# Two heads' key-value products in alternation on 64-column halves, with one shared 128-row tile for their last tokens

## The chip, the cores and the metric

The kernel runs on one core of a Trainium2 chip. The metric is device time in microseconds; the kernel before takes 1699.87 us, the median of three runs (1699.16 to 1702.06). Float32 throughout. TensorE (PE) multiplies and writes to PSUM, VectorE (DVE), ScalarE (ACT) and GpSimd (POOL) do the rest, and SyncE (SP) issues the transfers.

## The reference

Eight batches of eight heads with 576 tokens of 64 features go through a softmax attention without a score matrix, and its output through two layers:

```
q_s = exp(q - max(q over features));  q_s = q_s / (sum over features + 1e-9)
k_s = exp(k - max(k over tokens));    k_s = k_s / (sum over tokens + 1e-9)
kv  = k_s^T v            (64 x 64 for each batch and head, summed over 576 tokens)
x   = q_s kv             -> (4608 tokens, 512)
x   = relu(x w_in)^2 w_out      (512 -> 2048 -> 512)
out = silu(x w_in2) w_out2      (512 -> 2048 -> 512)
```

The change concerns `kv` alone: the product of the exponentials of k with v, and how the last 64 of the 576 tokens are laid out for it.

## The kernel before

Tokens go in nine blocks of 512, through the first layer block by block (phase 0) and then through the second (phase 1). In either phase a block has 16 slots, one for each chunk of 128 hidden features. `layer_in` (lines 397 to 404) makes the 12 products of a chunk of the first matrix, and `layer_out` (lines 448 to 470) those of the second, two chunks behind. All of these are float32r products of 128 rows, 128 columns and 512 moving columns.

The attention of batch and block b + 1 runs beside block b of phase 0, head pair by head pair. Pair 0 to 3 starts at slot 0, 4, 8 and 11: its k, q and v are loaded one slot earlier, the maximum over tokens and the exponential follow in slots 0 and 1 of its own, and `kv_mm` (lines 210 to 218) two slots behind the start. Batch 0 has all this ahead of the layers, in an order written out by hand (`first_loads`, `first_steps`), with its tiles in room that later weights take (`spare`). A scheduler then orders each engine's instructions, so neighbours in the code need not be neighbours on the engine.

`kv_load` (lines 148 to 175) lays the first 512 tokens of two heads on 128 partitions, 4 tokens each (`kk`), and the last 64 on 64 partitions, the two heads side by side (`krr`, 64 x 128). v has the same layout, with a column of ones behind each head's 64 features (`vv`, `vrr`), so that the product gives the sum of the exponentials too. `kv_max` takes the maximum over a partition's tokens, then over partitions on GpSimd (line 196); `kv_exp` subtracts it and takes exp (lines 201 to 206).

`kv_mm` sums a head's five products in one PSUM tile: four over 128 rows (line 216) and one over the 64 rows of the last tokens (line 217). Head 0 has PSUM partitions 0 to 63, which are TensorE's columns 0 to 63, head 1 the other half. Head 0's five go first, then head 1's. `kv_norm` follows on VectorE and ScalarE.

What sets the order around it: SyncE's queue runs in order, and from the ninth transfer on each waits for one issued eight earlier. GpSimd's queue runs in order as well. The k, v and last-token tiles of later batches have one buffer each, so loads and memsets of a pair wait for the products of the pair before. PSUM tiles of the attention share two buffers.

Of the kernel before, what the change touches and what calls it, by code (L numbers as in the profile page):

```python
# [19 lines left out]
def f32(ap):  # L20
    """A float32r tile's values, read as the float32 numbers that they are."""
    return ap.bitcast(F32)
# [3 lines left out]
def kernel(  # L26
# [10 lines left out]
):  # L37
    """softmax attention -> relu^2 layer -> silu layer, in float32.

    The weights come as the words of float64 numbers (zero, or of a size within float32's normal  # L40
    range) and are rounded to the nearest float32 here.

    A float32 x is the exact sum of two float32r numbers, hi = round(x) to 12 significant bits and
    lo = x - hi. The big products are hi*hi + hi*lo + lo*hi, each an exact one-pass product that
    PSUM sums in float32; lo*lo lies below float32's rounding.

    Tokens go in blocks of 512, as columns: column 128 * a + 32 * r + j of a block is its token
    128 * a + 4 * j + r, which softmax has on partition 32 * a + j.
    Activations stay transposed (features on partitions) until the last product.
    """  # L50
    nc = tc.nc
    P = 128
# [9 lines left out]
    SR = S - SM  # L62
    # (block, pair) whose q softmax leans on ScalarE, while the weights keep VectorE busy.
    ON_ACT = ((0, 0), (0, 1), (0, 2), (1, 0), (1, 1), (1, 2), (1, 3))
    EPS = 1e-9
    Q = 32
    # Blocks whose q goes through TensorE to be transposed.
    PE_TR = (0, 1)
# [22 lines left out]

# [1 line left out]
    w_in = (w_in1, w_in2)  # L93
# [20 lines left out]
    def round_w(ph, f, which):  # L114
        """float64 words -> the nearest float32's bits."""
        t = raw.pop((ph, f, which))
        lw, hw = t[:, :, 0], t[:, :, 1]
        u = tpool.tile([P, DM], I32, tag="wu", name="wu")
        nc.scalar.activation(lw, lw.bitcast(U32), AF.Copy, scale=2.0 ** -29)  # L119
        nc.vector.tensor_scalar(  # L120
            u, hw, 0x07FFFFFF, 3, op0=ALU.bitwise_and, op1=ALU.logical_shift_left
        )
        nc.vector.scalar_tensor_tensor(  # L123
            u, hw, -0x40000000, u, op0=ALU.bitwise_and, op1=ALU.bitwise_or
        )
        nc.vector.tensor_tensor(u, u, lw, op=ALU.add)  # L126
        raw[ph, f, which] = u
# [10 lines left out]

# [1 line left out]
    kt, krt, vt, vrt, mt, mbt = {}, {}, {}, {}, {}, {}  # L140

    def spare(pr, j):
        """Room of the last weights, which block 0's attention can have."""
        n = 6 * pr + j
        tag = f"wo{'hl'[n % 2]}{NF - 1 - n // 2}"
        return wpool.tile([P, TB], F32, tag=tag, name=f"spare{n}")

    def kv_load(b, pr):
        hs = slice(2 * pr, 2 * pr + 2)
        if b == 0:  # L150
            t = [spare(pr, j) for j in range(4)]
            kk, krr = t[0], t[3][0:SR, 0:2 * D]
            w = R * (D + 1)
            vv = [t[1][:, 0:w], t[2][:, 0:w]]
            vrr = t[1][0:SR, w:w + 2 * (D + 1)]
            m, mb = t[3][:, 2 * D:4 * D], t[3][:, 4 * D:6 * D]
        else:
            kk = apool.tile([P, TB], F32, tag="k", name="k")
            krr = apool.tile([SR, 2 * D], F32, tag="kr", name="kr")
            t = apool.tile([P, 2, R * (D + 1)], F32, tag="v", name="v")  # L160
            vv = [t[:, 0, :], t[:, 1, :]]
            vrr = apool.tile([SR, 2 * (D + 1)], F32, tag="vr", name="vr")
            m = apool.tile([P, 2 * D], F32, tag="m2", name="m2")
            mb = apool.tile([P, 2 * D], F32, tag="mb", name="mb")
        kk = kk.rearrange("p (h r d) -> p h r d", h=2, r=R)
        krr = krr.rearrange("p (h d) -> p h d", h=2)
        vv = [x.rearrange("p (r d) -> p r d", r=R) for x in vv]
        vrr = vrr.rearrange("p (h d) -> p h d", h=2)
        nc.sync.dma_start(out=kk, in_=k[b, hs, 0:SM, :].rearrange("h (p r) d -> p h r d", r=R))
        nc.sync.dma_start(out=krr, in_=k[b, hs, SM:S, :].rearrange("h p d -> p h d"))  # L170
        for j in range(2):
            nc.gpsimd.memset(vv[j][:, :, D:D + 1], 1.0)
        nc.gpsimd.memset(vrr[:, :, D:D + 1], 1.0)
        kt[b, pr], krt[b, pr], vt[b, pr], vrt[b, pr] = kk, krr, vv, vrr
        mt[b, pr], mbt[b, pr] = m, mb

    def v_load(b, pr):
        hs = slice(2 * pr, 2 * pr + 2)
        for j in range(2):
            nc.sync.dma_start(  # L180
                out=vt[b, pr][j][:, :, 0:D],
                in_=v[b, 2 * pr + j, 0:SM, :].rearrange("(p r) d -> p r d", r=R),
            )
        nc.sync.dma_start(
            out=vrt[b, pr][:, :, 0:D], in_=v[b, hs, SM:S, :].rearrange("h p d -> p h d")
        )

    def kv_max(b, pr):
# [5 lines left out]
        nc.vector.tensor_tensor(m2, m1[:, :, 0, :], m1[:, :, 1, :], op=ALU.max)  # L194
        nc.vector.tensor_tensor(m2[0:SR], m2[0:SR], tr, op=ALU.max)
        nc.gpsimd.partition_all_reduce(mb, m, P, bass_isa.ReduceOp.max)

    def kv_exp(b, pr):
# [4 lines left out]
        )  # L203
        nc.vector.tensor_tensor(tr, tr, mb[0:SR], op=ALU.subtract)
        nc.scalar.activation(t, t, AF.Exp)
# [4 lines left out]
    def kv_mm(b, pr):  # L210
        ps = ps_a.tile([P, D + 1], F32, tag="a", name="kvps")
        ek, ekr, va, vr = kt.pop((b, pr)), krt.pop((b, pr)), vt.pop((b, pr)), vrt.pop((b, pr))
        for j in range(2):
            o = ps[D * j:D * j + D]
            for r in range(R):
                nc.tensor.matmul(o, ek[:, j, r, :], va[j][:, r, :], start=(r == 0), stop=False)  # L216
            nc.tensor.matmul(o, ekr[:, j, :], vr[:, j, :], start=False, stop=True)  # L217
        kvps[b, pr] = ps
# [17 lines left out]
    def pieces(i):  # L236
        """(batch, first and last partition) of block i's tokens."""
        got, p = [], 0
# [62 lines left out]
    def q_tr(i, pr):  # L301
        t = qt.pop((i, pr))
        if i in PE_TR:
# [5 lines left out]
            return  # L309
        # VectorE transposes blocks of 32 x 32 in their place; a trip through DRAM orders them.  # L310
        u = t.rearrange("p h r d -> p (h r d)")
# [9 lines left out]
    def parts(t, p0, p1):  # L321
        """The columns of a block's tokens on partitions p0 to p1."""
        got = []
# [26 lines left out]
    def x_mm(i, pr):  # L350
        hi, lo = qht.pop((i, pr), None), qlt.pop((i, pr), None)
        got = []
        for b, s, p0, p1 in pieces(i):
# [4 lines left out]
            else:  # L358
                # A float32r product runs at full rate from 256 columns on.
                c0, c1 = p0 // Q * P, -(-p1 // Q) * P  # L360
# [9 lines left out]

# [1 line left out]
    xh = [xpool.tile([P, TB], F32R, name=f"xh{c}") for c in range(KC)]  # L372
# [20 lines left out]

# [1 line left out]
    gh, gl, gf, acc = {}, {}, {}, {}  # L395
# [29 lines left out]
    def evict(ph, i, e, last):  # L425
        """A finished accumulator to DRAM; the kernel's last ones in two halves side by side."""
        w = TB // 2 if last else TB
        for n in range(TB // w):
# [3 lines left out]
            if ph == 0:  # L432
                # Phase 1's columns: r * 128 + p for token 4 * p + r.
                to = t.rearrange("p (r a j) -> p a r j", r=R, j=Q)
                have = have.rearrange("p (a r j) -> p a r j", r=R, j=Q)
# [12 lines left out]
    def layer_out(ph, i, fn):  # L448
        """Adds the products of some chunks, (f, n) each, to block i's four accumulators."""
        ended = fn[-1][0] == NF - 1  # L450
# [20 lines left out]

# [1 line left out]
    side = {}  # L473
# [42 lines left out]
    items = [(ph, i, f) for ph in range(2) for i in range(NB) for f in range(NF)]  # L516
    # Each chunk's second product runs two chunks behind its first.
    order = []
# [14 lines left out]

    # Weights, (phase, chunk, in or out), in the order in which they are needed.
    wlist = [(0, 0, 0), (0, 1, 0)]
# [3 lines left out]

    # Block 0's attention and the first weights: a letter code and a pair (or a weight) each, loads  # L540
    # first, then the steps by their priority.
    code = dict(
# [39 lines left out]
    for what, n in order:  # L582
        ph, i, f = items[n]
        if what == "in":
# [14 lines left out]
            hidden_lo(n)  # L599
            # Phase 1's weights take the places of phase 0's as its last block lets them go.  # L600
            slot = n - (NB - 1) * NF
# [42 lines left out]
```

## Time and profile before

| what | value |
|---|---|
| median of three runs | 1699.87 us |
| span of the profiled execution | 1697.9 us |
| median less that span | 2.0 us |
| PE busy | 1671.6 us, 98% |
| DVE, ACT, POOL busy | 712.6, 606.0, 42.2 us |
| line 216, with the batches' own tiles | 448 records, 38.0 us |
| line 217, the same | 112 records, 18.2 us |
| first product on PE | 19.95 us |
| last product of line 217 | 710.4 us |

Busy times of PE overlap: a record covers the way of a product through the array, so the distance from one start to the next is what a product costs in a row, not its duration. A float32 product shows as two records of MATMUL and two of LDWEIGHTS (PEld, the load of the stationary operand). Shapes are rows times columns of the array used: 128*64 is 128 rows and half of the columns.

### The profile page before, as it was taken

To read this page: it belongs to the slowest core of one execution; us is meant where nothing else is said; L and a number is where in the kernel's file an instruction comes from. 1 tells how busy PE (TensorE), PEld (TensorE's weight loads), DVE (VectorE), ACT (ScalarE), POOL (GpSimd) and SP (SyncE) were. 2 spreads that over 40 slices of the span, in tenths; PEclk is the share of its full clock that TensorE was granted. 3 is DMA by queue.
4 is the path that set the end of the run, shared out by engine and by line. 5 is a ranking of instruction groups with operands and counts; after the bars stand their busy time and mean duration, and the time that the engine had idled before them with its cause. 6 is when DMAs were issued, how large, how long until landed. Compare 5 with 4: busy or idle time off the path is not lost.

```text
span 1697.9 us, 20340 instructions
## 1 busy us (share of the span) xinstructions
PE 1671.6 (98%) x7768; PEld 1373.7 (81%) x7768; DVE 712.6 (42%) x1393; ACT 606.0 (36%) x1186; POOL 42.2 (2%) x148
## 2 busy tenths in 40 slices
PE   5999999999999999999999999999999999999999
PEld 3878888888888888888887888888888888888887
DVE  6997565555656555553686121212121212121211
ACT  6785333332333233332565232223232323222222
POOL 1010000000000000000000000000000000000000
PEclk9999999999999999999999999999999999999999
DMA  6664221231222122120454010101010101010000
GB/s 178 199 202 131 73 72 52 57 93 54 77 66 73 57 70 77 37 81 13 126 170 138 0 50 0 50 1 50 0 50 0 50 1 50 1 50 1 15 11 25
DMA packets 119842, 106.19 MB, mean 63 GB/s; under 512 B 49600, under 2 KB 98752, under 8 KB 119744
## 3 DMA queue, kind: packets, MB, share of 16 engines
q1 hardware_dynamic: 119744, 104.89, 20.1%
q8 instruction: 61, 1.00, 0.2%
q14 instruction: 37, 0.30, 0.1%
HBM read 78.64 MB, written 26.21 MB: 62 GB/s over the span
## 4 chain that ended last, share of the span: by engine, by line
PE 94%; DVE 2%; DMA 2%; ACT 1%; issue 0%; SPq 0%; POOL 0%; DVEq 0%; ACTq 0%
PE acc L463 44%; PE h L401 15%; PE h L402 15%; PE h L403 15%; PE kvps L216 2%; DMA wraw<-in_moe_w_out_dram 1%; PE kvps L217 1%; PE xps L367 1%; PE xps L366 1%; PE xps L365 1%; DMA wraw<-in_moe_w_in_dram 0%; DVE wu L126 0%; DVE wu L123 0%; ACT wraw L119 0%; PE qps L307 0%
## 5 line engine op out<-in xcount | busy, mean ns | idle before, releaser
L422 DVE TENSOR_TENSOR gl<-g,gh 128x512 fp32r<-128x512 f32 x288 | 198.9, 691 | 637.8 <-ACT gh L417 635.3
L401 PE MATMUL h<-xh,wih 128*128 128x512 f32 x1152 | 448.5, 390 | 0.6 <-ACT g L416 0.6
L402 PE MATMUL h<-xl,wih 128*128 128x512 f32 x1152 | 449.0, 390 | 0.0
L403 PE MATMUL h<-xh,wil 128*128 128x512 f32 x1152 | 448.8, 390 | 0.0
L416 ACT ACTIVATE g<-h 128x512 f32<-128x512 f32 x144 | 86.1, 598 | 521.5 <-PE h L403 521.5
L401 PEld LDWEIGHTS h<-xh,wih 128*128 128x128 f32 x1152 | 216.0, 188 | 46.9 <-ACT g L416 1.0
L402 PEld LDWEIGHTS h<-xl,wih 128*128 128x128 f32 x1152 | 216.3, 188 | 45.6 <-DVE xl L378 0.4
L403 PEld LDWEIGHTS h<-xh,wil 128*128 128x128 f32 x1152 | 216.2, 188 | 45.6 <-DVE wil L135 0.4
L463 PE MATMUL acc<-gh,woh 128*128 128x512 f32 x576 | 228.0, 396 | 0.0
L463 PE MATMUL acc<-gl,woh 128*128 128x512 f32 x576 | 224.8, 390 | 1.0 <-DVE gl L422 0.9
L463 PE MATMUL acc<-gh,wol 128*128 128x512 f32 x576 | 224.7, 390 | 0.0
L463 PE MATMUL acc<-woh,gh 128*128 128x512 f32 x576 | 224.1, 389 | 0.0
L463 PE MATMUL acc<-wol,gh 128*128 128x512 f32 x576 | 224.1, 389 | 0.0
L463 PE MATMUL acc<-woh,gl 128*128 128x512 f32 x576 | 224.1, 389 | 0.0
L417 ACT CAST gh<-g 128x512 fp32r<-128x512 f32 x288 | 178.8, 621 | 60.1 <-DVE g L414 53.7
L410 ACT ACTIVATE g<-h 128x512 f32<-128x512 f32 x144 | 85.6, 594 | 260.4 <-PE h L403 259.9
L414 DVE TENSOR_TENSOR g<-g 128x512 f32<-128x512 f32 x112 | 77.3, 690 | 201.8 <-ACT g L410 201.1
L463 PEld LDWEIGHTS acc<-gh,woh 128*128 128x128 f32 x576 | 108.1, 188 | 23.0 <-ACT gh L417 0.3
L463 PEld LDWEIGHTS acc<-gh,wol 128*128 128x128 f32 x576 | 108.1, 188 | 22.8
L463 PEld LDWEIGHTS acc<-woh,gl 128*128 128x128 f32 x576 | 108.1, 188 | 22.6
L463 PEld LDWEIGHTS acc<-woh,gh 128*128 128x128 f32 x576 | 108.2, 188 | 22.4
L463 PEld LDWEIGHTS acc<-gl,woh 128*128 128x128 f32 x576 | 108.2, 188 | 22.4 <-DVE gl L422 1.8
(100 smaller groups left out, 1150.9 us busy)
## 6 DMA issues: line engine op xcount, KB each, us to landing
wraw<-in_moe_w_in_dram SPq DMA_DIRECT2D x32, 512.0 KB, 3.8
wraw<-in_moe_w_out_dram SPq DMA_DIRECT2D x32, 512.0 KB, 4.4
x2d<-ev SPq DMA_DIRECT2D x36, 256.0 KB, 2.1
xr<-x2d SPq DMA_DIRECT2D x36, 256.0 KB, 3.0
out_dram<-ev SPq DMA_DIRECT2D x32, 256.0 KB, 2.5
k<-in_k_dram SPq DMA_DIRECT2D x28, 256.0 KB, 2.8
v<-in_v_dram SPq DMA_DIRECT2D x56, 128.0 KB, 2.9
qd<-q SPq DMA_DIRECT2D x28, 256.0 KB, 2.0
```

The costliest lines, as they stand in the source:

```text
L216: nc.tensor.matmul(o, ek[:, j, r, :], va[j][:, r, :], start=(r == 0), stop=False)
L217: nc.tensor.matmul(o, ekr[:, j, :], vr[:, j, :], start=False, stop=True)
L365: nc.tensor.matmul(ps[:, o], wh, hi[:, o], start=True, stop=False)
L401: nc.tensor.matmul(h, wih[ph, f][o], xh[c], start=(c == 0), stop=False)
L402: nc.tensor.matmul(h, wih[ph, f][o], xl[c], start=False, stop=False)
L403: nc.tensor.matmul(h, wil[ph, f][o], xh[c], start=False, stop=(c == KC - 1))
L410: nc.scalar.activation(g, h, AF.Relu)
L414: nc.vector.tensor_tensor(g, g, g, op=ALU.mult)
L416: nc.scalar.activation(g, h, AF.Silu)
L417: nc.scalar.copy(hi, g)
L422: nc.vector.tensor_tensor(lo, gf.pop(n), f32(gh[n]), op=ALU.subtract)
L463: nc.tensor.matmul(acc[e], a, b, start=(f == 0 and j == 0), stop=(f == NF - 1 and j == 2))
```

## The change

The last 64 tokens of the two heads now share one tile of 128 partitions. v's has head 0 on partitions 0 to 63 and head 1 on 64 to 127, with one column of ones. k's has a block of 64 columns per head, and the other head's partitions in that block are filled with -3e38, which exp makes 0. So a head's product over all 128 rows adds nothing of the other head. Maxima, subtraction and exp run over all 128 partitions. Each of the two tiles is loaded by two transfers instead of one, and GpSimd fills the two padded quarters. In `kv_mm` the loop over the five products is the outer one now and that over heads the inner one. The rest of the textual difference is removed comments.

```diff
+    LOW = -3e38
...
         if b == 0:
-            kk, krr = t[0], t[3][0:SR, 0:2 * D]
+            kk, krr = t[0], t[3][:, 0:2 * D]
-            vrr = t[1][0:SR, w:w + 2 * (D + 1)]
+            vrr = t[1][:, w:w + D + 1]
...
-            krr = apool.tile([SR, 2 * D], F32, tag="kr", name="kr")
+            krr = apool.tile([P, 2 * D], F32, tag="kr", name="kr")
-            vrr = apool.tile([SR, 2 * (D + 1)], F32, tag="vr", name="vr")
+            vrr = apool.tile([P, D + 1], F32, tag="vr", name="vr")
...
+        for j in range(2):
+            nc.gpsimd.memset(krr[SR * j:SR * (j + 1), 1 - j, :], LOW)
         nc.sync.dma_start(out=kk, in_=k[b, hs, 0:SM, :].rearrange("h (p r) d -> p h r d", r=R))
-        nc.sync.dma_start(out=krr, in_=k[b, hs, SM:S, :].rearrange("h p d -> p h d"))
+        for j in range(2):
+            nc.sync.dma_start(out=krr[SR * j:SR * (j + 1), j, :], in_=k[b, 2 * pr + j, SM:S, :])
...
-        nc.gpsimd.memset(vrr[:, :, D:D + 1], 1.0)
+        nc.gpsimd.memset(vrr[:, D:D + 1], 1.0)
...
-        nc.sync.dma_start(
-            out=vrt[b, pr][:, :, 0:D], in_=v[b, hs, SM:S, :].rearrange("h p d -> p h d")
-        )
+        for j in range(2):
+            nc.sync.dma_start(
+                out=vrt[b, pr][SR * j:SR * (j + 1), 0:D], in_=v[b, 2 * pr + j, SM:S, :]
+            )
...
-        nc.vector.tensor_tensor(m2[0:SR], m2[0:SR], tr, op=ALU.max)
+        nc.vector.tensor_tensor(m2, m2, tr, op=ALU.max)
...
-        nc.vector.tensor_tensor(tr, tr, mb[0:SR], op=ALU.subtract)
+        nc.vector.tensor_tensor(tr, tr, mb, op=ALU.subtract)
...
-        for j in range(2):
-            o = ps[D * j:D * j + D]
-            for r in range(R):
-                nc.tensor.matmul(o, ek[:, j, r, :], va[j][:, r, :], start=(r == 0), stop=False)
-            nc.tensor.matmul(o, ekr[:, j, :], vr[:, j, :], start=False, stop=True)
+        for r in range(R + 1):
+            for j in range(2):
+                a, x = (ek[:, j, r, :], va[j][:, r, :]) if r < R else (ekr[:, j, :], vr)
+                nc.tensor.matmul(ps[D * j:D * j + D], a, x, start=(r == 0), stop=(r == R))
```

On PE, in block 1, the products of batch 2's first pair stand between `layer_in` (wih, wil) and `layer_out` (woh, wol) of a chunk. Before:

```order
L402 MATMUL h<-xl_129,wih_475 128x512
L403 MATMUL h<-xh_125,wil_476 128x512
L216 MATMUL kvps<-v,k 64x65 x4
L217 MATMUL kvps<-vr,kr 64x65
L216 MATMUL kvps<-v,k 64x65 x4
L217 MATMUL kvps<-vr,kr 64x65
L463 MATMUL acc_1713<-gh,woh_464 128x512
L463 MATMUL acc_1713<-gl,woh_464 128x512
```

The same place in the changed kernel, where the eight products over the first 512 tokens take the two heads in turn:

```order
L408 MATMUL h<-xl_129,wih_495 128x512
L409 MATMUL h<-xh_125,wil_496 128x512
L223 MATMUL kvps<-v,k 64x65 x8
L223 MATMUL kvps<-vr,kr 64x65 x2
L469 MATMUL acc_1749<-gh,woh_484 128x512
L469 MATMUL acc_1749<-gl,woh_484 128x512
```

The products of the last tokens stand together at the end now, and the whole keeps its place among the layers' products; so do all 24 pairs of batches 2 to 7.

On PE, in block 0, the last pair of batch 1, before:

```order
L463 MATMUL acc_617<-gl,woh_1257 128x512
L216 MATMUL kvps<-v,k 64x65 x4
L463 MATMUL acc_617<-gh,wol_1258 128x512
L217 MATMUL kvps<-vr,kr 64x65
L216 MATMUL kvps<-v,k 64x65 x4
L217 MATMUL kvps<-vr,kr 64x65
L463 MATMUL acc_618<-gh,woh_1257 128x512
```

And in the changed kernel:

```order
L469 MATMUL acc_636<-gh,woh_1367 128x512
L223 MATMUL kvps<-v,k 64x65 x8
L407 MATMUL h<-xh_122,wih_1378 128x512
L408 MATMUL h<-xl_126,wih_1378 128x512
L223 MATMUL kvps<-vr,kr 64x65 x2
L409 MATMUL h<-xh_122,wil_1379 128x512
```

Full-size products stand between the two parts of this pair in either kernel. Over batch 1's four pairs there are 6 such visits before (2, 1, 1 and 2) and 9 now (3, 2, 2 and 2).

## Rows read from the trace of the kernel before

**Rows 1.** The page's first part: busy time, share of the span, instructions.

```profile
PE 1671.6 (98%) x7768; PEld 1373.7 (81%) x7768; DVE 712.6 (42%) x1393; ACT 606.0 (36%) x1186; POOL 42.2 (2%) x148
```

**Rows 2.** The page's chain of work that ended last, by engine.

```profile
PE 94%; DVE 2%; DMA 2%; ACT 1%; issue 0%; SPq 0%; POOL 0%; DVEq 0%; ACTq 0%
```

**Rows 3.** Busy time by stretch: PE, PEld, DVE, ACT, POOL; clock, DMA share, GB/s.

```profile
120.00:230.00 110.00, 110.00 (x546) 90.11 (x545) 73.12 (x158) 46.84 (x89) 4.45 (x19) 1.00 0.35 101
...
670.00:780.00 110.00, 110.00 (x512) 90.59 (x512) 57.26 (x110) 36.22 (x68) 1.70 (x5) 1.00 0.18 57
```

**Rows 4.** The same view, a stretch of the first block.

```profile
60.00:80.00 20.00, 20.00 (x104) 16.35 (x103) 18.46 (x39) 16.49 (x43) 1.37 (x4) 1.00 0.59 191
```

**Rows 5.** PE's groups by form: count, busy us, mean ns, idle before.

```profile
L216 PE MATMUL kvps<-v,k 128*64 128x65 f32 x448 | 38.0, 227 | 0.2 <-issue 0.2
L217 PE MATMUL kvps<-vr,kr 64*64 64x65 f32 x112 | 18.2, 243 | 0.0
```

**Rows 6.** Timeline, one pair of batch 2: start us, us, engine, line, operation.

```profile
245.85 0.39 PE L402 MATMUL h<-xl,wih 128*128 128x512 f32 x1
...
246.07 0.39 PE L403 MATMUL h<-xh,wil 128*128 128x512 f32 x1
246.39 0.54 PEld L216 LDWEIGHTS kvps<-v,k 128*64 128x64 f32 x8 [0.35 <-issue]
246.39 0.68 PE L216 MATMUL kvps<-v,k 128*64 128x65 f32 x8
...
247.00 0.33 PE L217 MATMUL kvps<-vr,kr 64*64 64x65 f32 x2
...
247.26 0.68 PE L216 MATMUL kvps<-v,k 128*64 128x65 f32 x8
...
247.87 0.33 PE L217 MATMUL kvps<-vr,kr 64*64 64x65 f32 x2
...
248.12 0.50 PE L463 MATMUL acc<-gh,woh 128*128 128x512 f32 x1
...
248.69 0.39 PE L463 MATMUL acc<-gh,wol 128*128 128x512 f32 x1
```

**Rows 7.** The chain in order of time, a split pair of batch 1.

```profile
118.46 0.65 PE kvps L216 x8
119.11 0.43 PE acc L463
119.54 0.26 PE kvps L217 x2
```

**Rows 8.** PE's timeline, its first work (batch 0, first pair).

```profile
19.95 1.10 PE L216 MATMUL kvps<-spare,spare 128*64 128x65 f32 x8 [19.95 <-ACT spare L205]
20.97 0.47 PE L217 MATMUL kvps<-spare,spare 64*64 64x65 f32 x2
21.38 1.13 PE L216 MATMUL kvps<-spare,spare 128*64 128x65 f32 x8
```

**Rows 9.** POOL's timeline at the start.

```profile
0.73 0.14 POOL L172 MEMSET spare<- 128x4 f32 x2 [0.29 <-POOLq L627]
0.80 0.09 POOL L173 MEMSET spare<- 64x2 f32 x1
...
1.28 0.21 POOL L571 MEMSET kvf<- 128x128 f32 x1
...
17.52 2.23 POOL L196 PARTITION_ALL_REDUCE spare<-spare  x3 [6.46 <-issue]
```

**Rows 10.** SyncE's timeline at the start (SPq: an issue).

```profile
10.56 0.63 SPq L184 DMA_DIRECT2D spare<-in_v_dram  x1
...
15.05 0.59 SPq L101 DMA_DIRECT2D wraw<-in_moe_w_in_dram  x1
```

**Rows 11.** DVE's timeline: the second weight is taken up.

```profile
24.98 0.41 DVE L120 TENSOR_SCALAR wu<-wraw 128x512 int32<-128x512 int32 x1
```

**Rows 12.** Transfers of the first 40 us: count, size, median us to landing.

```profile
wraw<-in_moe_w_in_dram SPq DMA_DIRECT2D x4, 512.0 KB, 4.3
...
spare<-in_v_dram SPq DMA_DIRECT2D x4, 32.0 KB, 3.6
```

More of the change, by code (lines that the diff above doesn't have):

```diff
@@ L65 @@
     EPS = 1e-9
+    LOW = -3e38
+    assert 2 * SR == P
     Q = 32
@@ L167, in kv_load @@
         vv = [x.rearrange("p (r d) -> p r d", r=R) for x in vv]
-        vrr = vrr.rearrange("p (h d) -> p h d", h=2)
+        for j in range(2):
+            nc.gpsimd.memset(krr[SR * j:SR * (j + 1), 1 - j, :], LOW)
         nc.sync.dma_start(out=kk, in_=k[b, hs, 0:SM, :].rearrange("h (p r) d -> p h r d", r=R))
-        nc.sync.dma_start(out=krr, in_=k[b, hs, SM:S, :].rearrange("h p d -> p h d"))
+        for j in range(2):
+            nc.sync.dma_start(out=krr[SR * j:SR * (j + 1), j, :], in_=k[b, 2 * pr + j, SM:S, :])
         for j in range(2):
             nc.gpsimd.memset(vv[j][:, :, D:D + 1], 1.0)
-        nc.gpsimd.memset(vrr[:, :, D:D + 1], 1.0)
+        nc.gpsimd.memset(vrr[:, D:D + 1], 1.0)
         kt[b, pr], krt[b, pr], vt[b, pr], vrt[b, pr] = kk, krr, vv, vrr
@@ L177, in v_load @@
     def v_load(b, pr):
-        hs = slice(2 * pr, 2 * pr + 2)
         for j in range(2):
```

## The prediction

> **What bounds the kernel now.** I read the page first, by engine: TensorE (PE) is busy 98% of the span, VectorE 42%, ScalarE 36%, GpSimd 2% [rows 1]. The chain of work that ended last says the same, 94% of it on PE [rows 2]. Both are averages, so the table by stretches comes next: from 120 to 780 us, where the attention of the next batch runs beside the first layer, PE is busy 110.00 of every 110 us and VectorE 57 to 73 [rows 3]. Even in the first block, where the weights are rounded too, PE is full and VectorE stands at 18.46 of 20 us [rows 4]. So PE time removed between about 42 and 780 us is span removed, nearly one for one, and no other engine has to get faster for it.
>
> Then the rows of the touched lines. Line 216 has 512 MATMUL records (448 with the batches' own tiles, shown) and line 217 has 128 (112 shown) [rows 5]: 32 pairs of heads, 10 float32 products each, two passes to a product, 20 passes to a pair. The mean duration there (227, 243 ns) is useless as a price, since pipelined records overlap; starts are what counts. One undisturbed pair [rows 6]: the last full-size product starts at 246.07, then four runs start at 246.39, 247.00, 247.26 and 247.87, and the next full-size product at 248.12. Two runs of 8 passes take 0.61 each, two of 2 passes 0.255 on the mean. A straight line through these gives **p = 0.059 us per pass** ((0.61 - 0.255) / 6) and **s = 0.137 us per run** (0.255 - 2p). Four runs: 4 x 0.137 + 20 x 0.059 = 1.73, which is 248.12 - 246.39. So a run costs more than two passes before it does anything, and what starts a new run is the shape in the rows: 128*64 to 64*64 and back.
>
> A visit to this work costs something besides. From 246.07 to the third full-size start behind it, 248.69, is 2.62; three full-size steps (246.07 less the start before it, 245.85, hence 0.227) take 0.68 and the runs 1.73, which leaves **v = 0.21 us per visit** for leaving the full-size shape and coming back.
>
> **The change part by part.** *The runs.* All 20 passes of a pair now have 128 rows and 64 columns, so the shape changes only on entry and on exit: one run instead of four. The padded last tile costs no more passes (two per head, as before), and its 128 rows instead of 64 cost nothing in time per column: p fits both shapes above. What is new is that the output half changes after every product, 9 times a pair. No row shows a change of half without a change of shape. The nearest is from 247.00/247.26 [rows 6]: 217 of head 0 to 216 of head 1 changes both and takes as long (0.26) as 216 to 217, where the half stays. The half therefore added nothing that can be seen there. I take p for such a step; the bounds are half of p (both halves work at once) and p + s (it stalls like a change of shape). The saving is 3 x 0.137 = 0.41 us per pair. For batches 2 to 7, 24 pairs that stand in one piece before and after: **-9.8 us**.
>
> The Trainium skill, "TensorEngine Tiling (Array Packing)", Key Properties, says that a change of tiling mode, not merely of tile, drains TensorE. By that rule the three inner runs go and the nine half changes are free, which is the sum above; the s of the rows agrees with its first half, and no run here shows the second.
>
> *Batch 1* (its four pairs run in block 0). Here the order of the changed kernel is worse: the four pairs come in 9 visits instead of 6, since the late second transfer of the last k tokens makes the scheduler slip full-size products in between. Before: 16 runs, 6 visits, 80 passes: 16 x 0.137 + 6 x 0.21 + 80 x 0.059 = 8.17. Now: 9 runs, 9 visits: 9 x 0.137 + 9 x 0.21 + 4.72 = 7.84. **-0.3 us**. The trace has such a split at 118.46 to 119.54: 1.08 between two runs that lie 0.61 apart otherwise, less one full-size step of 0.227, is 0.24, near v [rows 7].
>
> *The start* (batch 0, before the layers run). PE's first work begins at 19.95 and waits till then for exp of the first pair [rows 8], behind it the subtraction and GpSimd's first maximum over partitions, at 17.52 [rows 9]. Gain: 12 runs fewer, 12 x 0.137 = 1.6, and a little more as the first pair is slow (runs of 1.02 and 0.41 [rows 8]; s is 0.21 there). PE takes turns with VectorE and ScalarE here, so I count half, -0.9. Loss: eight memsets more on GpSimd, whose queue runs in order, ahead of what it does before the first maximum. A 128x4 or 64x2 one costs under 0.1, a 128x128 one 0.21 [rows 9]; eight are 0.7 to 1.6, and I take 1.0. SyncE issues eight transfers more for batch 0, at 0.6 each in this stretch [rows 10]. The last tokens of v for the first pair, issued at 10.56 with four small transfers more ahead and one of their own, land at 10.56 + 5 x 0.62 + 3.6 = 17.3 [rows 10, 12], before 19.95. The second weight, issued at 15.05, has seven more ahead: 15.05 + 4.3 + 4.3 = 23.7 [rows 10, 12], and VectorE takes it at 24.98 [rows 11]. So they are hidden, by 1 to 3 us; if that cover is gone the start is some 2 us later. VectorE now has three subtractions ahead of the first reciprocal, part of the same 2 us. Net **+0.1**, between -2 and +4.
>
> *At nothing:* maxima, subtraction and exp of the last tokens run over 128 partitions instead of 64, with the same count per partition. In the steady part two more small transfers and two more memsets per pair lie on queues that are nearly empty (GpSimd 1.70 us busy from 670 to 780 [rows 3]); the memsets of a new tile wait for the previous pair's products, as those of v do now, and only that pair's maximum stands behind them, a slot later.
>
> **Sum:** -9.8 - 0.3 + 0.1 = -10.0 on a span of 1697.9. The median of the runs, 1699.87, lies 2.0 above the span, which I leave: **1689.9 us**. With p between 0.056 and 0.062 over 28 pairs of 20 passes (1.7 either way) and the start's bounds, this case reaches from 1686 to 1695.
>
> **The rivals.** *B, the halves really work at once.* The passes of one head run in the shadow of the other's. Two passes then cost one p; a pair saves another 10 x 0.059 = 0.59: 24 x 1.0 + 0.3 + 4 x 0.59 and about 1 at the start, 1672. If only the step from one head to the other overlaps (9 of 19), 1681. For it: nothing else uses the other 64 columns. Against it: each pass loads 64 columns of weights first, the loads take 0.54 of the 0.68 of a run of eight [rows 6], and the two passes of one product follow each other on the same half.
>
> The Trainium skill, "TensorE: Matmul & The Clock Gate", "What overlaps and what doesn't", states that a weight load overlaps running products only if its row group differs, and the two halves share theirs. By it B falls and the sum stays at A's; the rows speak for no such strict rule, as in [rows 6] loads and products of one half already overlap.
>
> *C, taking turns costs what the runs gave back.* If the weights for the other half can't be loaded ahead, every change of half shows part of s. Break-even is 0.41 / 9 = 0.046 us, a third of s. Around it the change doesn't do what it says: at 0.03 to 0.06 a pair changes by -0.14 to +0.13, together 1696 to 1703, about 1700.
>
> *D, a change of half stalls like a change of shape* (slower). Nine times s, 1.23, against 0.41 saved: +0.82 per pair, 24 x 0.82 = 19.7; batch 1 nearly 5 (some of its changes fall on splits), the start about 2: +26, 1726. It decides from the same 0.046. Against it: the step at 247.26, which changes the half too and costs no more than one that doesn't [rows 6].
>
> **How the numbers follow.** A 0.64, B 0.14, C 0.09, D 0.13. The forecast is A's. A measurement here tells from no change what is over 0.2%, 3.4 us. Faster than that: A, B and a little of C, 0.80; within it: most of C, 0.06; slower: D and an edge of C, 0.14. The range reaches over C above and nearly all of B below, 1674 to 1701; left out are D and the end of B, under 0.2.
>
> **What would show it.** In the timeline a pair should be one run of 20 of about 1.32 us instead of 1.73, with the step into the next full-size product unchanged; records of the line 640 as before. Under B the run is 0.7 to 1.0, under C 1.7, under D about 2.5. Batch 1's four pairs should show nine visits. The first product should start at 20 to 22 us, and the stretches from 120 to 780 should still show PE at 110 of 110. I would be wrong if PE showed idle time before the products of the last tokens (a late transfer or memset), if the start were more than 4 us later, or if the step between heads were not p.

## The result and the profile after

The changed kernel takes 1675.85 us (median of four, 1674.87 to 1677.17) against 1700.96 for the kernel before (four runs of the two occasions together): a ratio of 0.9855, 95% interval 0.9841 to 0.9869. The profiled execution's span is 1673.1 us against 1697.9. The time lies in the stated range and moved in the forecast direction, but the gain is 25 us where 10 were forecast: between batches 2 and 7 rival B came true. B's own total, 1672, lies below the range; the time stays inside it because some 3 us of B's gain are lost early, as shown below, and that is luck.

The page's first part and the chain's shares, which answer to [rows 1] and [rows 2]:

```profile
PE 1642.4 (98%) x7768; PEld 1348.8 (81%) x7768; DVE 712.9 (43%) x1393; ACT 606.6 (36%) x1186; POOL 49.8 (3%) x212
...
PE 88%; DVE 2%; DMA 2%; ACT 1%; issue 0%; DVEq 0%
```

PE still bounds, with the same 7768 records and 29.2 us less busy time. Its share of the chain is 88% where it was 94%, and its idle time, span less busy time, is 30.7 us against 26.3; by single records 23.8 and 20.5 of that fall in the first 36 us. The groups of the products (now all on line 223), as [rows 5] had them for lines 216 and 217:

```profile
L223 PE MATMUL kvps<-v,k 128*64 128x65 f32 x448 | 19.6, 227 | 0.0
L223 PE MATMUL kvps<-vr,kr 128*64 128x65 f32 x112 | 8.2, 226 | 0.0
```

There are as many records, each about as long on the mean (227 and 226 ns against 227 and 243), but they take half the time: 27.8 us together against 56.2. They must lie on top of each other. The pair at the place of [rows 6] in the timeline (it stands in block 2, so it is batch 3's, there and here):

```profile
241.37 0.39 PE L409 MATMUL h<-xh,wil 128*128 128x512 f32 x1
241.69 0.69 PE L223 MATMUL kvps<-v,k 128*64 128x65 f32 x16
242.20 0.29 PE L223 MATMUL kvps<-vr,kr 128*64 128x65 f32 x4
242.42 0.50 PE L469 MATMUL acc<-gh,woh 128*128 128x512 f32 x1
```

From 241.69 to 242.42 the 20 passes take 0.73 us, where they took 1.73. Record by record, in all 24 pairs of batches 2 to 7, the starts come in twos, 6 or 7 ns apart, and the twos follow each other at 0.055 to 0.061 us, but for the first step of 0.107. By the prediction's own terms that is s + 10p = 0.137 + 0.59 = 0.73: the price of B. The steps into the run and out of it have not changed.

Where the time went, counted by the starts of the layers' full-size products in the two profiled executions (product 360 is the first one behind all of batch 1's attention, product 2660 lies behind the last batch's):

| full-size product | before, us | changed kernel, less before |
|---|---|---|
| 0 | 31.89 | +0.2 |
| 120 | 68.29 | +0.3 |
| 360 | 133.97 | -0.6 |
| 1060 | 312.93 | -7.6 |
| 2660 | 724.43 | -24.3 |
| 6911, the last | 1693.53 | -24.9 |

Of the 24.9 us, 23.7 come from the 24 pairs of batches 2 to 7, at 0.99 each. The start and batch 1, eight pairs, give 0.6 in all. The last 0.6 fall at the change from the first layer to the second, near 900 us. PE's idle time there is nearly the same (1.59 us before, 1.54 now), so where these 0.6 come from is not shown. A second profiled execution of the changed kernel has +0.5, -0.3, -24.0 and -24.6 at products 0, 360, 2660 and 6911.

### The profile page after: what moved, and what is told of

It is laid out like the page before. It is cut to its first block, busy times and chain, and to the rows that moved or that the text cites. A ratio compares the mean times of both kernels' runs of the same rounds, so it can differ in the third digit from the quotient of the medians.

```text
span 1673.1 us, 20547 instructions
## 1 busy us (share of the span) xinstructions
PE 1642.4 (98%) x7768; PEld 1348.8 (81%) x7768; DVE 712.9 (43%) x1393; ACT 606.6 (36%) x1186; POOL 49.8 (3%) x212
## 4 chain that ended last, share of the span: by engine, by line
PE 88%; DVE 2%; DMA 2%; ACT 1%; issue 0%; DVEq 0%
PE acc L469 43%; PE h L407 14%; PE h L408 14%; PE h L409 14%; DMA wraw<-in_moe_w_out_dram 1%; PE kvps L223 1%; DVE wu L125 1%; DVE wu L128 1%; DMA wraw<-in_moe_w_in_dram 1%; PE xps L373 1%; PE xps L372 0%; PE xps L371 0%; DVE wu L122 0%; ACT g L418 0%; ACT wraw L121 0%
## 5 line engine op out<-in xcount | busy, mean ns | idle before, releaser
L469 PEld LDWEIGHTS acc<-wol,gh 128*128 128x128 f32 x576 | 108.2, 188 | 22.4
```

What stands on the lines that cost most here:

```text
L469: nc.tensor.matmul(acc[e], a, b, start=(f == 0 and j == 0), stop=(f == NF - 1 and j == 2))
```

## Which part does it: heads one by one, turns without padding

The first experiment keeps the padded tile and puts the loops back in the old order:

```diff
-        for r in range(R + 1):
-            for j in range(2):
+        for j in range(2):
+            for r in range(R + 1):
```

> The changed kernel with the loops of the products in the old order: padded tile, all five products of head 0, then all five of head 1. Theory 1 (the halves work at once only where neighbours in the queue are on different halves): a pair's run of 20 passes takes 0.137 + 20 x 0.059 = 1.32 us instead of 0.73, 24 pairs x 0.59 = +14, about 1690 us. Rival, theory 2 (PE looks far ahead in its queue and fills the idle half whatever the order): 0.73 to 0.8 us, about 1676.

It takes 1688.38 us, ratio 0.9934 (0.9919 to 0.9949). A pair of batch 2 in its timeline:

```profile
197.43 0.74 PE L223 MATMUL kvps<-v,k 128*64 128x65 f32 x10
197.94 0.22 PE L223 MATMUL kvps<-vr,kr 128*64 128x65 f32 x1
198.00 0.22 PE L223 MATMUL kvps<-v,k 128*64 128x65 f32 x1
198.00 0.22 PE L223 MATMUL kvps<-vr,kr 128*64 128x65 f32 x1
198.06 0.45 PE L223 MATMUL kvps<-v,k 128*64 128x65 f32 x5
198.35 0.28 PE L223 MATMUL kvps<-vr,kr 128*64 128x65 f32 x2
198.56 0.50 PE L469 MATMUL acc<-gh,woh 128*128 128x512 f32 x1
```

The run takes 198.56 - 197.43 = 1.13 us, between the two theories and nearer the first. How it falls short of 1.32 stands in the order of the rows. In the program head 0's eight passes on v,k and two on vr,kr come first, then head 1's. The rows show ten passes on v,k before the first on vr,kr: two of head 1's had started while two of head 0's were still waiting, and one more follows between those two. All 24 pairs of batches 2 to 7 show this order. PE takes up passes for the idle half past passes that wait for the busy one, about three ahead. Three passes hidden are 3 x 0.059 = 0.18, and 1.32 less 0.18 is 1.14. So theory 1 holds with a short reach ahead, and theory 2 falls.

Padding alone, then, saves 1.73 - 1.13 = 0.60 a pair: 0.41 for the three runs, as forecast, and 0.18 for the passes that slip past the change of head. In the kernel before, where a change of shape lies there, none did: its 1.73 is four runs in full.

The second takes the new order alone, on the kernel before:

```diff
-        for j in range(2):
-            o = ps[D * j:D * j + D]
-            for r in range(R):
-                nc.tensor.matmul(o, ek[:, j, r, :], va[j][:, r, :], start=(r == 0), stop=False)
-            nc.tensor.matmul(o, ekr[:, j, :], vr[:, j, :], start=False, stop=True)
+        for r in range(R + 1):
+            for j in range(2):
+                o = ps[D * j:D * j + D]
+                a, x = (ek[:, j, r, :], va[j][:, r, :]) if r < R else (ekr[:, j, :], vr[:, j, :])
+                nc.tensor.matmul(o, a, x, start=(r == 0), stop=(r == R))
```

> The kernel before with the loops of the products in the new order alone: no padding, the last tokens of a head as a product of 64 rows. Theory (turns give the large part, padding saves one run): two runs a pair, 2 x 0.137 + 10 x 0.059 = 0.86 us against 0.73, 24 x 0.137 = +3.3 on the changed kernel, about 1679; the start can be up to 1.5 earlier, as eight memsets and eight transfers fall away. Rival (both are needed: products of 64 rows don't work at once, or the change of shape costs more when both halves are busy): 1.0 us a pair or more, 1682 or more.

```profile
192.33 0.69 PE L217 MATMUL kvps<-v,k 128*64 128x65 f32 x16
192.94 0.33 PE L217 MATMUL kvps<-vr,kr 64*64 64x65 f32 x4
193.21 0.50 PE L463 MATMUL acc<-gh,woh 128*128 128x512 f32 x1
```

Two runs, 193.21 - 192.33 = 0.88 us a pair, as expected; the products of 64 rows work at once too. The total is 1677.06 us (0.9869, 0.9854 to 0.9883), hardly more than the changed kernel's, although 24 pairs lose 0.146 each, 3.5 us. It makes most of them good early: its product 360 starts 3.4 us earlier than in the kernel before, against 0.6 in the changed one. So the loops are nearly the whole gain, and padding gives and takes about the same; the intervals of the two ratios overlap.

## How far PE looks, and what it looks for

Turns of two products, with the padded tile:

```diff
-        for r in range(R + 1):
-            for j in range(2):
+        for rs in ((0, 1), (2, 3), (4,)):
+            for j in range(2):
+                for r in rs:
```

> The changed kernel with turns of two products (two of head 0, two of head 1, two, two, one, one). Theory 1 (only neighbours overlap): of the 19 steps only those at a change of head, five, are hidden: 1.32 - 5 x 0.059 = 1.03 us a pair, +7 us, about 1683. Theory 2 (PE looks ahead): 0.73 to 0.8 us a pair, about 1676.

```profile
196.39 0.73 PE L224 MATMUL kvps<-v,k 128*64 128x65 f32 x16
196.91 0.34 PE L224 MATMUL kvps<-vr,kr 128*64 128x65 f32 x4
197.18 0.50 PE L470 MATMUL acc<-gh,woh 128*128 128x512 f32 x1
```

197.18 - 196.39 = 0.79 us, 1677.92 in all (0.9872, 0.9857 to 0.9887). Strict neighbours would have given 1.03. In a group of four passes one is under way and three wait, which is as far as the first experiment showed PE to reach, so here theory 2's number comes out within that bound. The same reach explains the changed kernel: each float32 product is two passes on one half, and the other half's first pass starts past the second of these.

The control: both heads' products over the first 512 tokens still take turns, but on the same half, in a PSUM tile twice as wide.

```diff
+        w = D + 1
...
-                nc.tensor.matmul(ps[D * j:D * j + D], a, x, start=(r == 0), stop=(r == R))
+                if r < R:
+                    o = ps[0:D, w * j:w * j + w]
+                    nc.tensor.matmul(o, a, x, start=(r == 0 and j == 0), stop=False)
+                else:
+                    nc.tensor.matmul(ps[D * j:D * j + D, 0:w], a, x, start=(j == 1), stop=True)
```

> The changed kernel in its new order, but the products over the first 512 tokens of both heads go to output half 0, head 1's into other columns of the same PSUM tile; only the products of the last tokens use both halves. Head 1's sum over the first 512 tokens is thereby left out of what follows. Theory (two passes run at once only if they are on different halves): 16 passes one after the other and four in pairs, 0.137 + 16 x 0.059 + 2 x 0.059 = 1.2 us a pair, +0.47 x 24 = +11, about 1687. Rival (it is enough that two independent sums take turns): 0.73 us, about 1676.

```profile
197.53 1.09 PE L226 MATMUL kvps<-v,k 128*64 128x65 f32 x15
198.40 0.27 PE L228 MATMUL kvps<-vr,kr 128*64 128x65 f32 x1
198.45 0.22 PE L226 MATMUL kvps<-v,k 128*64 128x65 f32 x1
198.50 0.28 PE L228 MATMUL kvps<-vr,kr 128*64 128x65 f32 x3
198.72 0.50 PE L474 MATMUL acc<-gh,woh 128*128 128x512 f32 x1
```

198.72 - 197.53 = 1.19 us against 0.73, and 1690.85 in all (0.9945, 0.9931 to 0.9958). Two independent sums that take turns are not enough; they need different halves. The one pass on half 1 that shows before the sixteenth on half 0 has again gone past three.

The last of this group gives each head's last tokens their own 64 partitions instead of the padding (head 1's on 64 to 127):

```diff
-                a, x = (ek[:, j, r, :], va[j][:, r, :]) if r < R else (ekr[:, j, :], vr)
+                h = slice(SR * j, SR * (j + 1))
+                a, x = (ek[:, j, r, :], va[j][:, r, :]) if r < R else (ekr[h, j, :], vr[h])
```

> The changed kernel, but the product of the last tokens takes each head's own 64 partitions (head 1's on 64 to 127, with output half 1), so that the padding is loaded but not used; the memsets stay. If a change of shape costs s once and the two quadrants work at once: 0.86 us a pair as without padding, about 1679. If the change of row half costs another s: 1.0 us a pair, about 1682.

```profile
195.03 0.69 PE L224 MATMUL kvps<-v,k 128*64 128x65 f32 x16
195.65 0.33 PE L224 MATMUL kvps<-vr,kr 64*64 64x65 f32 x4
195.91 0.50 PE L470 MATMUL acc<-gh,woh 128*128 128x512 f32 x1
```

It shows 195.91 - 195.03 = 0.88 us a pair, the same as without padding, so two opposite quarters of the array work at once and the change of row half costs nothing more. With the changed kernel's loads and memsets its product 360 is only 0.2 us ahead of the kernel before, and the total 1681.17 (0.9895, 0.9878 to 0.9911): the later gain of the second experiment without its early one. That points at the loads and memsets of the padded tile for what is lost early.

## What the start and batch 1 lost

The products of eight early pairs got cheaper as well, but the changed kernel has only 0.6 us of it at product 360. Two experiments add to the version without padding one of the two companions of the padded tile each: loads of the last tokens in two parts,

```diff
-        nc.sync.dma_start(out=krr, in_=k[b, hs, SM:S, :].rearrange("h p d -> p h d"))
+        for j in range(2):
+            nc.sync.dma_start(out=krr[:, j, :], in_=k[b, 2 * pr + j, SM:S, :])
```

(and the same for v),

> Without padding, products in the new order, and the last tokens' tiles of k and v loaded by two transfers each, as in the changed kernel. Theory L (two-part loads move the order of batch 1's products into more visits, and delay): product 360 gains under 1 us on the kernel before, total about 1680. Rival M (the memsets are the cost): 3.5 us there, total about 1677, as without padding.

and memsets of two quarters that nothing reads:

```diff
+        for j in range(2):
+            nc.gpsimd.memset(krr[SR:P, D * j:D * (j + 1)], -3e38)
+        krr = krr[0:SR].rearrange("p (h d) -> p h d", h=2)
```

> Without padding, products in the new order, one load for the last tokens of two heads, and GpSimd fills two quarters that nothing reads, as many bytes as the padding. Theory L: as without padding, product 360 gains 3.5 us on the kernel before, about 1677. Rival M (memsets ahead of the first maximum and of each pair's): under 1 us there, about 1680.

| version | product 0 | 120 | 360 | total, us |
|---|---|---|---|---|
| no padding | -0.8 | -2.1 | -3.4 | 1677.06 |
| and loads in two parts | -0.8 | -0.1 | +0.9 | 1680.01 |
| and memsets | +1.3 | +0.3 | -0.3 | 1679.33 |
| changed kernel | +0.2 | +0.3 | -0.6 | 1675.85 |

(Starts of full-size products in one profiled execution each, less the kernel before.) At product 360 either companion by itself takes the 3 us away, so both theories look half right. The totals are weaker evidence. Less the kernel before as it ran beside them, the three versions gain 23.0, 21.1 and 21.8 us, and the intervals of their ratios overlap (0.9854 to 0.9883, 0.9862 to 0.9895, 0.9862 to 0.9891).

The two companions act at different places. With memsets the first maximum on GpSimd begins at 19.59 instead of 17.95, and what stands behind it is late. But this time varies from one execution to the next: it lies between 17.64 and 19.59 in the seven profiled executions with the memsets in batch 0, between 16.52 and 18.41 in the six without, and is 0.8 later on the mean. With loads in two parts it begins at 16.52, and PE starts earlier, but then waits:

```profile
18.96 1.65 PE L217 MATMUL kvps<-spare,spare 128*64 128x65 f32 x20 [18.96 <-DMA spare<-in_v_dram]
20.54 1.12 PE L307 MATMUL qps<-ident,xr 128*128 128x128 f32 x4
24.24 2.91 PE L307 MATMUL qps<-ident,xr 128*128 128x128 f32 x12 [2.59 <-ACT kvf L229]
```

The changed kernel has the same gap, 2.79 us, before the same transposes:

```profile
21.72 1.12 PE L313 MATMUL qps<-ident,xr 128*128 128x128 f32 x4
25.63 2.91 PE L313 MATMUL qps<-ident,xr 128*128 128x128 f32 x12 [2.79 <-ACT kvf L235]
```

In the kernel before it is 0.24 us, without padding 0.81, and 2.79 again in the second profiled execution of the changed kernel. The cause is the order on VectorE and ScalarE. The version without padding keeps the order of the kernel before in all but a few places. In the changed kernel q of batch 0's third pair comes as the 22nd transfer, issued at 13.58, instead of the 17th at 11.23, and VectorE takes this q's maximum behind three subtractions of `kv_exp`. In the kernel before it stood ahead of them:

```profile
14.24 0.67 DVE L267 TENSOR_REDUCE mx<-spare 128x8 f32<-128x512 f32 x1
```

In the changed kernel:

```profile
21.59 0.68 DVE L273 TENSOR_REDUCE mx<-spare 128x8 f32<-128x512 f32 x1
23.18 0.15 DVE L230 RECIPROCAL rc<-rc 128x1 f32<-128x1 f32 x1
...
22.30 0.35 ACT L276 ACTIVATE spare<-spare,mx 128x64 f32<-128x64 f32 x1
...
24.63 0.33 ACT L276 ACTIVATE spare<-spare,mx 128x64 f32<-128x64 f32 x1
...
24.96 0.62 ACT L235 ACTIVATE kvf<-kvps,rc 64x64 f32<-64x64 f32 x2
```

ScalarE's eight exponentials of this q, from 22.30 on, so come ahead of `kvf`, the first pair's normalized product. Its reciprocal is ready at 23.33, 1.6 us before `kvf` starts. The version with loads in two parts has the same order.

Batch 1's products, too, come in nine visits instead of six in both. From product 0 to product 360 the three profiled executions with the old tile and one load in batch 1 and without added memsets (no padding, and twice the version from batch 2 on below) gain 2.2 to 3.0 us, and the three with the padded one (the changed kernel twice, and the version from batch 1 on) 0.2 to 0.8. So about 2 of the 3 us are lost in batch 1's stretch. How much of these is the visits is not shown.

The way out is the old tile of the last tokens where the order was tuned to it, and the padded one behind it. In each place of the layout stands a condition like this one, with `PAD = 2` and, for comparison, 1:

```diff
-        for j in range(2):
-            nc.gpsimd.memset(krr[SR * j:SR * (j + 1), 1 - j, :], LOW)
+        if b >= PAD:
+            for j in range(2):
+                nc.gpsimd.memset(krr[SR * j:SR * (j + 1), 1 - j, :], LOW)
```

> The products in the new order everywhere; the padded tile with its memsets and two-part loads from batch 2 on alone, batches 0 and 1 with the old 64-row tile and one load. Theory (the padded tile's loads and memsets cost the start and batch 1 about 3 us, and save 0.146 us a pair later): product 360 of the layers starts 3.5 us earlier than in the kernel before, as without padding anywhere, against 0.3 in the changed kernel, and every later pair still saves 1.0: 1672.5 us. Rival (the 3 us are the luck of one run, or the mix of two layouts brings waits of its own): about 1676.

> The same with the old tile for batch 0 alone. If the loss lies in batch 0's loads, before the layers begin: the first full-size product starts 1 us earlier than in the kernel before, and the total is near 1673. If it lies in batch 1, whose pairs come in ten visits here: product 360 gains under 1.5 us on the kernel before, total about 1675.

From batch 2 on: 1673.05 us (0.9834, 0.9820 to 0.9849), product 0 at -0.3 and product 360 at -2.5. From batch 1 on: 1674.70 (0.9848, 0.9833 to 0.9863), product 0 at -1.2 and product 360 at -1.4. That fits a share gained before the layers begin and another lost in batch 1's nine visits (the trace shows nine, not the ten of the expectation). But batch 0 has the same tiles in both versions and their product 0 still differs by 0.9, so one execution of each doesn't show it. As the intervals of these versions and of the changed kernel overlap, it and the better one ran once more, side by side:

> The changed kernel as it is, beside the next one on the same chip: about 1675.9.

> The version with the old tile of the last tokens for batches 0 and 1, beside the changed kernel on the same chip. If its earlier start is worth what product 360 showed (2.4 against 0.3), it is 1 to 2.5 us faster than the changed kernel; if that was one run's luck, the same.

1675.07 us (1674.62 to 1677.61) for the changed kernel and 1673.24 (1672.09 to 1673.71) for padding from batch 2 on, with no run of one among those of the other; against the kernel before 0.9856 (0.9842 to 0.9869) and 0.9841 (0.9828 to 0.9855). It is some 2 us faster than the changed kernel and the fastest of all that ran. Its product 360 is at -4.0 in this execution and was at -2.5 in the one above, so a single early start is good to about 1.5 us. Its start:

```profile
19.45 1.65 PE L237 MATMUL kvps<-spare,spare 128*64 128x65 f32 x20 [19.45 <-ACT spare L224]
21.03 1.12 PE L327 MATMUL qps<-ident,xr 128*128 128x128 f32 x4
22.95 3.12 PE L327 MATMUL qps<-ident,xr 128*128 128x128 f32 x12 [0.81 <-ACT kvf L249]
```

## Why the prediction was right or wrong

*The bound: right.* PE time was span. The 24 pairs' visits got 1.00 us shorter each, 0.99 of it came off the span, and in the stretch from 340 to 450 us PE is still full:

```profile
340.00:450.00 110.00, 110.00 (x563) 90.85 (x562) 64.98 (x140) 38.42 (x76) 6.40 (x25) 1.00 0.24 70
```

*The price of a run: right.* s of 0.137 for a change of shape and p of 0.059 for a pass, read off starts in [rows 6], account for the changed kernel's 0.73, for 0.88 with two runs (2s + 10p = 0.86) and for 1.19 on one half (s + 18p = 1.20).

*The step between heads: wrong, and this is the miss.* The sum took p for it, between bounds of half p and p + s. In the trace the 20 passes cost 10p: each pass of one head lies beside one of the other. Even the lower bound was too high, as half a p less at nine steps is 0.27 us a pair and 0.59 came off. The term "3 x 0.137 = 0.41 us per pair" measured 1.00. Over 24 pairs the 0.59 left out is 14.2 us, nearly all of the 14.8 by which the span fell further than the 10.0 forecast. Two arguments against B in the prediction failed. "The two passes of one product follow each other on the same half" is true, but PE does not keep to the program's order between the halves: it starts the other half's pass past as many as three that wait. And that the weight loads fill most of the run, 0.54 of 0.68 in [rows 6], does not bind, since loads for the two halves overlap as well:

```profile
241.69 0.55 PEld L223 LDWEIGHTS kvps<-v,k 128*64 128x64 f32 x16 [0.35 <-issue]
```

Sixteen loads in the 0.55 us that eight took before. The Trainium skill, "TensorE: Matmul & The Clock Gate", "What overlaps and what doesn't", on which the prediction drew against B, says that loads overlap running products only in another row group and that products start in strict order; here both differ, and the measurement decides. What I had to weigh it with lay at hand: the rows showed loads overlapping products of the same half, against the rule's first part, and I should have given B more than 0.14.

*The start and batch 1: the sum came near (-0.2 forecast, -0.6 and -0.3 measured in two executions), by luck and not by its terms.* The first product on PE began at 20.34 instead of 19.95, but at 20.38 in the version without padding, which has none of the added memsets: one execution doesn't show the memsets' delay, taken as 1.0; on the mean of those profiled it is 0.8. Cheaper products gave about 3 there, as the version without padding shows, which is also near the 3.7 that B counted for them. The engines' order took that back. I had seen three subtractions ahead of the reciprocal and counted them in a bound, but what held `kvf` was ScalarE, with eight exponentials of q ahead of it: a wait of 2.8 us.

*C and D: excluded.* They put a pair at 1.7 and 2.5 us, and it took 0.73: a change of half adds nothing here.

## What to carry to other kernels

If two small products use 64 columns of TensorE each, put them next to one another in the program, on different output halves: here that made 20 passes cost what 10 did. Keep a run of such products in one shape, and count runs and visits by the distance between starts, not by durations. In a kernel whose order is tuned, even memsets or a transfer cut in two can cost about as much as the products save there, so change the layout where PE alone sets the pace and leave it elsewhere.

## What the runs showed of the hardware

Two passes on the two column halves of TensorE, when the halves take turns product by product, start 6 or 7 ns apart and take one pass's time, 0.059 us for 65 columns in float32, weight loads included, with 128 rows or with 64, and also in opposite quarters of the array. On one half the same turns take 1.19 us a pair instead of 0.73. PE's products do not start in program order when they use different halves: a pass went past three earlier ones that waited for the other half, with heads one by one and in the control on one half. None went past more there, and which limit sets these three isn't shown.
